# Three scheduling edits to a spectral-mixing and windowed-attention kernel: when the output projection's operands are prepared and where they live, which queue reads the row maxima, and the order in which a matrix piece is split

## The chip, the cores and the metric

One Trainium2 chip, one of its cores. The metric is device time in microseconds (us) of one execution. The times listed for the kernel before are 786.25, 770.50 and 777.87 us, median 777.87 us; the execution that was profiled took 772.52 us.

## What is computed (the reference, cut)

```python
# S = 2048 rows, D = 512 columns, 32 heads of 16, window W = 256
g = sigmoid((x * gate_w).sum(-1, keepdims=True))          # one gate per row
a = Cr @ (x @ Wr.T) - Ci @ (x @ Wi.T)                     # real part of a 2-D DFT
q, k, v = split(x @ wqkv)                                 # 32 heads
scores = (q @ k.T) * 16 ** -0.5                           # query i sees keys i-255 .. i
p = softmax(where(mask, scores, -1e9))
b = (p @ v) @ wo
out = g * a + (1 - g) * b
```

All of it is float32. A matmul of full precision is made of three in the faster float32r type: each operand is split into a high part (a cast) and a low part (operand minus high part), and high x high, high x low and low x high are accumulated (`TERMS`).

## The kernel before, in words

**One program order, written out by hand.** Every instruction is issued where the Python code calls it; each engine and each DMA queue works through its own instructions in that order. Two things are interleaved: the attention loop at the bottom of the function (`for n in range(N + LAG + 1)`), and a generator `dense()` that yields after each dense matmul (projections, then the DFT's products). `fill(n)` lets the generator advance by `rate / 2` steps, twice for each of the four head slots `p` of a turn `n`: 5 steps a turn once the projections are done (`FILL_SEQ`), 11 before (`FILL_PROJ`). Small work is postponed with `defer(ticks, fn, ...)`: a heap is emptied as a counter advances by 1 at each dense matmul, by 0.7 at each head slot, by 9 after each `pv`.

**The attention.** Heads come in 8 groups of 4, each with 16 row blocks, so 128 block turns. At turn `n` the kernel computes scores of block `n` (`s_head`, L442) and lets VectorE take the masked row maxima (L445); nine turns later (`LAG`), at `k = n - 9`, it computes the transposed scores (`t_head`, L497), in which the maxima are already subtracted because they sit as two extra rows (high and low part) in the tile `ring[0]`, and ScalarE exponentiates them (L498). GpSimd clears what lies outside the window (`t_mask`, L504 and L508). Every fourth turn `pv` multiplies by the values (L523), ScalarE copies one half of the sums out (L529), VectorE adds the other (L530). The scores of both kinds and these sums share four PSUM buffers (tag `st`).

**The row maxima's way.** Every fourth turn `m_rows(u)` (called here a unit, `u` counting from -3 to 29) splits 16 columns of maxima and transposes them on VectorE (L452 to L455); 2 ticks later SyncE's queue writes them to DRAM (`m_scr<-mt`), and 12 ticks after that reads them back as rows (`ring<-m_scr`, two or four DMAs a unit, 80 in all). In these 14 ticks falls the `pv` of the turn with its 9 ticks. Every load goes through `ld`, SyncE's queue (L97 in the profile); ScalarE issues a handful at the start only. DMAs take one of 8 semaphores in turn, so that each also waits for the landing of the one eight places before it.

**The normalizer's way.** After the last group of a half (groups 3 and 7) the sums and their row sums go out to DRAM (`o_out`), are packed (`o_pack`: `l_scr<-u_scr`, `o_scr<-u_scr`), the row sums read (`l_in`), inverted (`l_inv`) and written back (`l_back`), each step `d = 40` ticks after the one before. A set of four row blocks, 512 rows, is `sb` (0 to 3); the second half of `sb` is finished by `pv` 28 + `sb`, the last four of the attention.

**The DFT's last product.** 32 blocks, `c_block(n)`, each 12 matmuls with a piece of `cr` (n below 16) or `ci`. A piece is loaded three blocks ahead (`piece_load`: `raw`, `big`, and for odd rows `hl`) and split two blocks ahead (`piece_split`): the high part `hi` by ScalarE (L103), two differences on GpSimd (L328, L331) and one on VectorE, then the low part on GpSimd (L106), at ticks 0, 0, 2, 4 and 6. The differences feed only a check (`magnitudes`, L566; `guard`). The high part lies in a tile `es`, the low part in half of a tile `hl`.

**The output projection.** When the attention's loop is over, `attention_done` calls `o_prep(0)`: for each of four groups `o_load` reads inverted row sums (`rl<-l_scr`) and sums (`pt<-o_scr`), 256 KB each; 36 ticks later VectorE multiplies them (L830), ScalarE casts, VectorE subtracts. `o_prep(1)` comes 50 ticks later, `o_prep(2)` and `o_prep(3)` when `sb` 0 and 1 have been used. The results lie in the tiles `pt`, the products in `RL`, which takes the place of `ring[1]`. `wo` is loaded in four parts (`wo_load`): 0 and 1 at `n` = 18 and 19, 2 and 3 in `attention_done`. `wo_run` multiplies one of 16 row blocks (12 matmuls), once after each `c_block` if all is prepared, else at the very end.

## Time and profile before

| | before |
|---|---|
| median of the three times, us | 777.87 (770.50 to 786.25) |
| the profiled execution, us | 772.52 |
| its span (first to last instruction), us | 770.8 |
| mean granted clock of TensorE in it | 0.906 |
| instructions | 18841 |
| DMA: moved, mean rate | 174.36 MB, 226 GB/s |
| HBM read, written | 114.03 MB, 63.46 MB |

The profile names an engine's busy time (PE is TensorE, PEld its weight load, DVE VectorE, ACT ScalarE, POOL GpSimd, SPq the DMA queue of SyncE), and for a group or a single instruction the idle time before it with what ended it: `[3.75 <-DMA ring<-m_scr]` is 3.75 us of idling that ended when that DMA landed. Times in a timeline are us from the first instruction; tiles are written as what is written `<-` what is read. The attention's last matmuls run at 669 us; the first block of the DFT's last product begins at 353 us.

### The profile page before, as it was taken

Reading aid. Unit: us, or ns where it says so; the run is one execution under the profiler, and the core shown is the slowest. Engines: PE = TensorE matmul, PEld = TensorE weight load, DVE = VectorE, ACT = ScalarE, POOL = GpSimd, SP = SyncE. Lnnn points to the kernel's source line nnn. Section 1 sums busy time; section 2 is a strip of 40 time slices with the busy share of each in tenths; the row PEclk is TensorE's granted clock in tenths of the full one; section 3 lists DMA queues with packets and bytes.
Section 4 is the critical chain, followed back from the end, with each engine's and each line's share of the span. In section 5 each row is a group of like instructions: output and inputs, shape, how many; then the busy total and the mean of one; then the engine's idle time right before and its main releaser. Section 6 shows DMA issues by size and latency. Waiting matters only on the chain.

```text
span 770.8 us, 18841 instructions
## 1 busy us (share of the span) xinstructions
PE 650.1 (84%) x6558; PEld 499.8 (65%) x6558; DVE 544.1 (71%) x1471; ACT 437.8 (57%) x928; POOL 470.4 (61%) x718
## 2 busy tenths in 40 slices
PE   9999999899999999978677978878887687835976
PEld 6788887777788777766455655655555456624754
DVE  5388878898897889768567757676678863516554
ACT  6334775455576545666577657656756567514230
POOL 5002565667667878787768859796875869822000
PEclk9999999999999999989789879978978868975979
DMA  7857775777666877798868678885877648697675
GB/s 281 264 171 221 221 233 174 214 215 219 212 206 194 236 211 216 251 277 251 254 182 248 220 203 248 263 247 148 269 205 242 209 162 301 233 297 259 189 249 155
DMA packets 99994, 174.36 MB, mean 226 GB/s; under 512 B 34420, under 2 KB 35316, under 8 KB 99764
## 3 DMA queue, kind: packets, MB, share of 16 engines
q1 hardware_dynamic: 98452, 170.98, 72.2%
q10 hardware_dynamic: 1440, 2.10, 0.8%
q8 instruction: 54, 0.88, 0.5%
q14 instruction: 48, 0.39, 0.2%
HBM read 114.03 MB, written 63.46 MB: 230 GB/s over the span
## 4 chain that ended last, share of the span: by engine, by line
DMA 18%; PE 17%; POOL 8%; DVE 8%; issue 6%; SPq 4%; ACT 3%; DVEq 0%; POOLq 0%; ACTq 0%
DMA ring<-m_scr 5%; PE d L238 5%; SPq L97 4%; PE t L234 4%; DVE sm L445 3%; PE o L523 3%; DMA raw<-cr 3%; DMA ring<-qk_scr 3%; PE t L497 2%; DMA pt<-o_scr 2%; PE s L442 2%; POOL pt L504 1%; POOL hl L106 1%; DMA hl<-cr 1%; DMA ev<-wo 1%
## 5 line engine op out<-in xcount | busy, mean ns | idle before, releaser
L445 DVE CUSTOM_DVE_ANT_0 sm<-s,mask 128x384 f32<-128x384 f32 (+2 forms) x512 | 269.8, 527 | 87.0 <-PE s L442 41.9
L498 ACT ACTIVATE pt<-t 128x384 f32<-128x384 f32 (+2 forms) x512 | 234.2, 475 | 131.8 <-PE t L497 93.7
L497 PE MATMUL t<-ring,ring 50*128 50x384 f32 (+2 forms) x512 | 199.9, 400 | 56.6 <-DMA ring<-m_scr 32.0
L442 PE MATMUL s<-ring,ring 48*128 48x384 f32 (+2 forms) x512 | 185.0, 372 | 24.2 <-DVE nm L445 22.5
L504 POOL TENSOR_SCALAR_AFFINE_SELECT pt<-pt 128x256 f32<-128x256 f32 x256 | 116.0, 454 | 124.2 <-ACT pt L498 117.0
L238 PE MATMUL d<-big,hl 64*128 64x512 f32 x896 | 171.8, 421 | 0.0
L497 PEld LDWEIGHTS t<-ring,ring 50*128 50x128 f32 x512 | 101.9, 202 | 89.0 <-issue 26.5
L442 PEld LDWEIGHTS s<-ring,ring 48*128 48x128 f32 x512 | 99.4, 198 | 78.7 <-DVE nm L445 66.3
L238 PE MATMUL d<-hl,big 64*128 64x512 f32 x984 | 147.9, 395 | 0.0
L238 PE MATMUL d<-big,es 64*128 64x512 f32 x448 | 122.7, 473 | 0.0
L238 PEld LDWEIGHTS d<-big,hl 64*128 64x128 f32 x896 | 110.0, 198 | 5.2 <-issue 0.6
L238 PEld LDWEIGHTS d<-hl,big 64*128 64x128 f32 x984 | 105.2, 186 | 6.9 <-issue 0.8
L508 POOL TENSOR_SCALAR_AFFINE_SELECT pt<-pt 128x256 f32<-128x256 f32 x224 | 95.3, 425 | 0.0
L523 PE MATMUL o<-pt,vpad 64*32 64x320 f32 (+5 forms) x2816 | 83.3, 373 | 5.9 <-DVE nm L445 3.7
L523 PEld LDWEIGHTS o<-pt,vpad 64*32 64x32 f32 x2816 | 66.6, 113 | 28.1 <-DVE nm L445 10.3
L238 PEld LDWEIGHTS d<-big,es 64*128 64x128 f32 x448 | 66.3, 224 | 2.5 <-issue 0.6
L106 POOL TENSOR_TENSOR hl<-es,hl 128x512 fp32r<-128x512 f32 x14 | 19.0, 1359 | 65.2 <-ACT hl L103 61.6
L529 ACT COPY os<-o 128x512 f32<-128x512 f32 x32 | 18.8, 587 | 64.2 <-PE o L523 64.2
L530 DVE TENSOR_TENSOR os<-o,os 128x512 f32<-128x512 f32 x32 | 22.1, 690 | 42.8 <-ACT os L529 38.8
L106 POOL TENSOR_TENSOR hl<-raw,es 128x512 fp32r<-128x512 f32 x32 | 44.0, 1375 | 0.0
L243 ACT ACTIVATE es<-d 128x512 f32<-128x512 f32 x53 | 31.7, 598 | 19.8 <-PE d L238 19.0
L106 POOL TENSOR_TENSOR big<-big 128x512 fp32r<-128x512 f32 x32 | 41.6, 1304 | 0.2 <-ACT big L103 0.2
(100 smaller groups left out, 902.5 us busy)
## 6 DMA issues: line engine op xcount, KB each, us to landing
qk_scr<-hl SPq DMA_DIRECT2D x32, 512.0 KB
ring<-qk_scr SPq DMA_DIRECT2D x128, 128.0 KB
ring<-qk_scr SPq DMA_DIRECT2D x128, 64.0 KB
u_scr<-os SPq DMA_DIRECT2D x32, 256.0 KB
raw<-cr SPq DMA_DIRECT2D x16, 512.0 KB
big<-cr SPq DMA_DIRECT2D x16, 512.0 KB
raw<-ci SPq DMA_DIRECT2D x16, 512.0 KB
big<-ci SPq DMA_DIRECT2D x16, 512.0 KB
```

The source lines that it names most:

```text
L97: nc.sync.dma_start(dst, src)
L106: (nc.gpsimd if pool else nc.vector).tensor_sub(lo, raw, f(hi))
L234: nc.tensor.matmul(pss[0], w, x, start=start, stop=stop)
L238: nc.tensor.matmul(pss[h], w[r], x[r], start=start, stop=stop)
L243: nc.scalar.activation(t, pss[0], AF.Copy, scale=scale)
L442: nc.tensor.matmul(ps[:, :w], ring[0][r, p, jb * P:(jb + 1) * P], ring[1][r, p, k0:k0 + w], start=True, stop=True)
L445: nc.vector.tensor_tensor_reduce(out=sm[:, :w], in0=ps[:, :w], in1=mask[:, WIN - w:], scale=1.0, scalar=3e38, op0=OP.add, op1=OP.min, accu ...
L497: nc.tensor.matmul(ps[:, :w], ring[1][r, p, q0:q0 + P], ring[0][r, p, q0:q0 + w], start=True, stop=True)
L498: nc.scalar.activation(pt[:, j, :w], ps[:, :w], AF.Exp, scale=-1.0)
L504: nc.gpsimd.affine_select(a, a, pattern=[[0, 2], [1, P]], compare_op=OP.is_ge, fill=0.0, base=0, channel_multiplier=-1)
L508: nc.gpsimd.affine_select(a, a, pattern=[[0, 2], [-1, P]], compare_op=OP.is_gt, fill=0.0, base=0, channel_multiplier=1)
L523: nc.tensor.matmul(ot[h][32 * j:32 * j + 32, a - sb * 512:e - sb * 512], v2[r, j], pt[r, j, a - kb * P:e - kb * P], start=kb == kbs[0], st ...
```

## The change

1. The two or four reads of the maxima in each unit are issued by ScalarE's queue (`nc.scalar.dma_start`) instead of SyncE's.
2. In the second half of the normalizer's way the steps are 14 ticks apart instead of 40, and `l_back` calls `o_prep(sb)` at once. For `sb` 1 and 2 that waits until the attention is over; for `sb` 0 it happens in the attention, for `sb` 3 without a further condition.
3. `sb` 0 and 3 use tiles `big` for their results and `es` for the row sums; `sb` 1 and 2 keep `pt` and `RL`. The four groups of a set are loaded 9 ticks apart instead of 5, and multiplied 16 ticks after the load instead of 36.
4. All four parts of `wo` go into `big` tiles; parts 2 and 3 are loaded at `n` = 27 and 28. `wo_run` waits until all four have been split.
5. In `piece_split` the low part comes right after the high part (tick 2), the differences at ticks 4, 6 and 8; the high part lies in the other half of the `hl` tile, and `es` is free of it.

```diff
@@ m_rows, read
-                    ld(f(ring[0][64 * h + 48:64 * h + 50, :, b % NB * P:b % NB * P + (e - b) * P]),
-                       ms[:, h, :, o:o + e - b].rearrange("l p b i q -> l p (b i q)"))
+                    nc.scalar.dma_start(f(ring[0][64 * h + 48:64 * h + 50, :, b % NB * P:b % NB * P + (e - b) * P]),
+                                        ms[:, h, :, o:o + e - b].rearrange("l p b i q -> l p (b i q)"))
@@ pv
-        d = 40
+        d = 14 if hf else 40
...
             have.add(("o", sb, hf))
+            if hf:
+                o_prep(sb)
@@ piece_split
-        hi = ev.tile([P, 512], F32R, name="es", bufs=3)
         w = st.tile([P, 2, 512], F32R, name="hl")
+        hi = w[:, 1]
         defer(at_, hi_of, hi, main)
         for k, j in enumerate((2, 1, 3)):
             d, src, sign = left(i, tb, raws, j)
-            defer(at_ + step * k, minus if sign > 0 else plus, d, d, src, j != 3)
-        defer(at_ + step * 3, lo_of, w[:, 0], main, hi, True)
+            defer(at_ + step * (k + 2), minus if sign > 0 else plus, d, d, src, j != 3)
+        defer(at_ + step, lo_of, w[:, 0], main, hi, True)
@@ dense
-            if n in (18, 19):
-                wo_load(n - 18)
+            if n in (18, 19, 27, 28):
+                wo_load({18: 0, 19: 1, 27: 2, 28: 3}[n])
@@ wo_load
-        if g < 2:
-            t = big.tile([P, 2, 512], F32R, name="big")
-            d = [t[:, a] for a in range(2)]
-        elif g == 2:
-            d = [const.tile([P, 512], F32R, name=f"wo{a}", tag=f"vpad{a}") for a in range(2)]
-        else:
-            d = [const.tile([P, 512], F32R, name="wo2", tag="vpad2"), at.tile([P, 512], F32R, name="os", bufs=1)]
+        t = big.tile([P, 2, 512], F32R, name="big")
+        d = [t[:, a] for a in range(2)]
...
-        WO.append(d)
+        defer(34, WO.append, d)
@@ attention_done
-        o_prep(0)
-        defer(10, wo_load, 2)
-        defer(15, wo_load, 3)
-        defer(50, o_prep, 1)
         for tb in range(3):
-            defer(40, wo_get, tb)
+            defer(1 + 6 * tb, wo_get, tb)
@@ o_prep
-        if sb > 3:
-            return
-        if ("o", sb, 1) not in have:
+        if sb in (1, 2) and not FIN:
             return defer(6, o_prep, sb)
         OHL[sb] = []
         for g in range(NG):
-            defer(5 * g, o_load, sb, g)
+            defer(9 * g, o_load, sb, g)
@@ o_load
-        t = pt_tile([P, 3, 512], F32R)
         ls = l_scr[sb][g // 2]
-        rl = RL[0][:, sb % 2 * 2 + g // 2, g % 2]
+        if sb in (1, 2):
+            t = pt_tile([P, 3, 512], F32R)
+            rl, o = RL[0][:, sb % 2 * 2 + g // 2, g % 2], f(t[:, 2])
+        else:
+            t = big.tile([P, 2, 512], F32R, name="big")
+            rl, o = ev.tile([P, 512], F32, name="es", bufs=3), f(t[:, 1])
         ld(rl, bass.AP(tensor=ls.tensor, offset=ls[1, g % 2 * 8].offset, ap=[[512, 8], [0, 16], [1, 512]]))
-        ld(f(t[:, 2]), o_scr[sb][g])
+        ld(o, o_scr[sb][g])
...
-            nc.vector.tensor_mul(rl, f(t[:, 2]), rl)
+            nc.vector.tensor_mul(rl, o, rl)
...
-            defer(24, OHL[sb].append, t)
-        defer(36, product)
+            defer(8, OHL[sb].append, t)
+        defer(16, product)
@@ wo_run
-        if tb > 15 or len(OHL.get(sb, ())) < NG:
+        if tb > 15 or len(OHL.get(sb, ())) < NG or len(WO) < 4:
             return tick()
...
-        if c == 3:
-            o_prep(sb + 2)
```

## The prediction

> **What bounds the kernel now.** I read the page's busy times first, then a table by stage, then the waits, and last the timelines at the places where the change acts.
>
> ```profile
> span 770.8 us, 18841 instructions
> PE 650.1 (84%) x6558; PEld 499.8 (65%) x6558; DVE 544.1 (71%) x1471; ACT 437.8 (57%) x928; POOL 470.4 (61%) x718
> ```
>
> No engine is busy throughout, so the answer differs by stage. In the table a row is a stretch, its length, then the busy time of PE, PEld, DVE, ACT and POOL, the granted clock, the DMA engines' share and GB/s:
>
> ```profile
> 250.00:300.00 50.00, 46.09 (x563) 37.85 (x551) 42.62 (x114) 26.85 (x57) 41.31 (x64) 1.00 0.74 219
> 500.00:550.00 50.00, 39.54 (x349) 25.83 (x346) 37.06 (x103) 32.77 (x77) 38.99 (x57) 0.83 0.78 220
> 640.00:660.00 20.00, 14.03 (x159) 10.84 (x157) 6.02 (x7) 13.68 (x32) 18.15 (x25) 0.83 0.85 299
> 680.00:700.00 20.00, 6.47 (x14) 3.88 (x14) 3.46 (x6) 4.51 (x10) 7.51 (x6) 0.59 1.00 322
> ```
>
> While projections and attention run together, TensorE is the bound: 46.1 of 50 us, clock 1.00. In the second part every engine has slack and waits for another. At the attention's end GpSimd is the bound (18.2 of 20). Behind it TensorE does 6.5 us of work in 20 while the DMA engines are full. The waits name what the change addresses; the columns are us in total, times, longest:
>
> ```profile
> PE t L497 <- DMA ring<-m_scr: 32.0, 12, 7.0
> SPq L97 <- DMA m_scr<-mt: 18.6, 14, 3.2
> ```
>
> TensorE stood 32.0 us for maxima, all in the second part (the first such wait, 4.44 us, is quoted below), and SyncE's queue stood for the landing of the maxima's write before it could issue their read.
>
> **Term 1: the stretch behind the attention.** TensorE there (a bracket is the idle time before the row):
>
> ```profile
> 666.57 2.42 PE L523 MATMUL o<-pt,vpad 64*32 64x64 f32 x96
> ...
> 682.38 1.22 PE L234 MATMUL d<-big,es 128*128 128x512 f32 x2 [6.63 <-ACT es L103]
> 686.88 0.80 PE L234 MATMUL d<-big,hl 128*128 128x512 f32 x1 [3.27 <-POOL hl L106]
> ...
> 696.70 1.22 PE L234 MATMUL d<-big,es 128*128 128x512 f32 x2 [5.80 <-ACT es L103]
> 701.53 0.80 PE L234 MATMUL d<-big,hl 128*128 128x512 f32 x1 [3.61 <-POOL gl L618]
> ...
> 707.61 2.93 PE L234 MATMUL t<-big,pt 128*128 128x512 f32 x6
> ...
> 731.00 0.39 PE L234 MATMUL t<-wo,pt 128*128 128x512 f32 x1
> ...
> 742.00 2.76 PE L234 MATMUL t<-big,pt 128*128 128x512 f32 x6
> ...
> 754.04 0.79 PE L234 MATMUL t<-wo,pt 128*128 128x512 f32 x2 [0.38 <-DVE pt L106]
> ```
>
> Blocks 28 and 29 of the DFT run at once, 30 waits to 682.4 and 31 to 696.7 for their pieces; then eight blocks of the projection in 23.8 us (707.61 to 731.39, 2.97 each), then the ninth, which takes until 742.00. In blocks 30 and 31 the low part comes late, because GpSimd does two differences first:
>
> ```profile
> 681.75 1.27 POOL L331 TENSOR_TENSOR raw<-raw 128x512 f32<-128x512 f32 x1 [8.61 <-DMA raw<-ci]
> 683.82 1.77 POOL L328 TENSOR_TENSOR big<-big,hl 128x512 f32<-128x512 f32 x1 [0.81 <-DMA hl<-cr]
> 685.56 1.26 POOL L106 TENSOR_TENSOR hl<-raw,es 128x512 fp32r<-128x512 f32 x1
> ```
>
> - Low part first: waits of 3.27 and 3.61 shrink to about 1.3 (one GpSimd subtraction behind the cast): -4.3.
> - With `sb` 0 ready and part 3 of `wo` split 34 ticks after block 28 begins, the first `wo_run` that works stands at the end of block 30: 2.97 us fall into the wait for piece 31. -3.
> - `sb` 2 is loaded beside `sb` 1 right after the attention, some 40 us before its use. The ninth block took 10.6 us (731.39 to 742.00) and would take 2.97: -7.6. The smaller hold for `sb` 3 (0.38 in the last row, with the others about it some 1.4): -1.4.
> - Fewer restarts at the low clock (0.59 in that row): -2.7.
>
> The pieces come no sooner. SyncE's queue:
>
> ```profile
> 671.05 0.33 SPq L97 DMA_DIRECT2D u_scr<-os  x1
> ...
> 675.98 0.37 SPq L97 DMA_DIRECT2D raw<-ci  x1
> ...
> 687.52 0.36 SPq L97 DMA_DIRECT2D raw<-ci  x1
> ```
>
> The loads of `sb` 0 leave this place (2 MB, 6.5 us at 322 GB/s), but those of `sb` 1 and 2 now stand there, and `l_back` followed at once by `o_prep` makes the queue wait for the landing of `l_scr<-lt`. I count piece 30 as 2 to 3 us later, 31 unchanged. Sum -19; -30 if both pieces come with the freed bandwidth, -6 if they come later still.
>
> **Term 2: ScalarE waits for the write, first part.** The read stands 12 ticks behind the write, and nine of these are `pv`'s, so on ScalarE it falls one or two exponentials behind the copy of the `pv` sums. Unit 4 of 33, and with it the last of the 14 units that I followed between 76 and 309 us:
>
> ```profile
> 162.50 0.53 SPq L97 DMA_DIRECT2D m_scr<-mt  x1
> ...
> 166.04 0.55 SPq L97 DMA_DIRECT2D ring<-m_scr  x2
> ```
>
> ```profile
> 163.63 0.49 ACT L498 ACTIVATE pt<-t 128x384 f32<-128x384 f32 x1 [0.25 <-PE s L442]
> 164.72 0.49 ACT L498 ACTIVATE pt<-t 128x384 f32<-128x384 f32 x1 [0.59 <-PE t L497]
> ...
> 305.64 0.49 ACT L498 ACTIVATE pt<-t 128x384 f32<-128x384 f32 x1
> ```
>
> ```profile
> 166.52 0.34 PE L497 MATMUL t<-ring,ring 50*128 50x384 f32 x1
> ...
> 308.58 0.68 SPq L97 DMA_DIRECT2D ring<-m_scr  x2
> ```
>
> And of unit 13:
>
> ```profile
> 324.81 0.49 ACT L498 ACTIVATE pt<-t 128x384 f32<-128x384 f32 x1
> ...
> 333.97 1.55 SPq L97 DMA_DIRECT2D ring<-m_scr  x4
> ...
> 336.75 0.66 PE L497 MATMUL t<-ring,ring 50*128 50x384 f32 x1 [4.44 <-DMA ring<-m_scr]
> ```
>
> The queue read at 166.04, the moment the write had landed. ScalarE would be at the read at 164.12 and stand until 166.0, issue for 0.5, and start at 166.5 the exponential that began at 164.72. TensorE's scores at 166.52, which need a PSUM buffer that a later exponential frees, come at 168.2: 1.6 us late. In the last unit ScalarE is there at 306.13 and waits to 308.5. Over the 14 units it waits 29 us, and TensorE's next scores come 24 us late. Unit 13 adds a wait of 8.7 us (325.3 to 334.0) and unit 14 one of about 5, of which TensorE keeps some 9, since it stands there for 4.4 us already. So 33; VectorE, 42.6 of 50, uses the pauses to catch up, and 3.9 us of idling in 50 is all that can be made up from. I take 25, bounds 8 and 43 (the upper with a lowered clock behind each pause).
>
> **Term 3: the maxima land sooner, second part.** Of the 32.0 us, 26 lie behind 355 us. Two reads on today's queue, from the chain of waits, bound a landing:
>
> ```profile
> 394.26 5.55 DMA ring<-m_scr
> ...
> 473.27 1.59 DMA ring<-m_scr
> ```
>
> ```profile
> 504.37 0.81 ACT L498 ACTIVATE pt<-t 128x384 f32<-128x384 f32 x2
> ...
> 507.76 0.57 SPq L97 DMA_DIRECT2D ring<-m_scr  x2
> ```
>
> ```profile
> 515.00 0.66 PE L497 MATMUL t<-ring,ring 50*128 50x384 f32 x1 [3.75 <-DMA ring<-m_scr]
> ```
>
> In unit 22 ScalarE is free at 505.2, the write has landed by 506.5, and a read of 1.6 us is there before 509: the 3.75 us vanish. But ScalarE runs late in this part, and in half of these units it reaches the read 1 to 4 us behind SyncE's queue. At 1.6 us a landing, 17 of the 26 us go; at 5.55 none, and some 4 are added. With the loads of a DFT piece just ahead of it on the one queue and none on the other, the short landing is nearer. Since what follows meets the next wait (32.8 and 39.0 of 50 us on ACT and POOL), -14; bounds -25 and +4.
>
> The Trainium skill speaks against this term: "DMA: Bandwidth & Descriptors", section "Issuing engines are not separate DMA queues", says that issuing from several engines saves only the sequencer's time to start a transfer, as all run on the same 16 DMA engines. By that the reads land as late as now and the sum is 14 higher. The same page, section "Queues, rings and completion order", has each engine alternate between queues packet by packet, which speaks for the short landing; no row here decides.
>
> **Term 4: what is added in the attention.** For `sb` 0 eight loads (2 MB), four products and low parts on VectorE, four casts on ScalarE, and SyncE's queue waits for `l_scr<-lt` and for the fourth `es` tile. VectorE has room there (6.0 of 20 us), which hides them; GpSimd has none (18.2 of 20), and its subtraction took 1.77 instead of 1.27 us beside VectorE (683.82 above). With the DMA at 0.85 already, +4; 0 to 10. The differences that now come later delay ScalarE's `magnitudes` by a subtraction; that is in it. The other edits (tiles, `d`) cost nothing of their own.
>
> **Sum.** -19 + 25 - 14 + 4 = -4 on the profiled execution's 772.5 us (1.7 of it outside the span): 768.5 us. The median of the runs shown, 777.9, lies 5.4 higher, so I count from the profiled one, which is near the lowest.
>
> **Rivals.**
> - *ScalarE's wait is mostly absorbed.* Once delayed, it meets the writes later, and VectorE, which sets when they are written, has caught up. Term 2 falls to 8, term 3 reaches -18, term 1 -21, term 4 +3: 744.5 us. For: in the second part ScalarE mostly comes after the landing. Against: the rows of unit 4, with VectorE not behind.
> - *Slower: ScalarE's wait in front of the exponentials decides.* Place: the read behind `pv`. Price: 43 in term 2, and shorter waits in the second part become ScalarE's (-8). With -15 and +6: 798.5 us. It decides once TensorE's pauses pass 2 us a unit, so that the clock falls, 1.00 until now. For: TensorE has 3.9 us of slack in 50. By the Trainium skill, "TensorE: Matmul & The Clock Gate", Part 1, an idle window of about 3.4 us halves the clock; the trace agrees as far as it goes (0.83 where waits reach 7.0 us, 1.00 where there are none), and pauses of 2 us would be too short for it.
> - *The reads land as late as before* (term 3 at 0): 782.5 us.
> - *The tail doesn't do what it says*: the loads of `sb` 1 and 2 push piece 31 and the projection back as those of `sb` 0 and 1 do now; term 1 at -6: 781.5 us.
>
> **How the numbers follow.** Forecast 0.40, the rivals in order 0.26, 0.16, 0.11, 0.07. A measurement of this kernel tells about 2% from no change: below 757.1 or above 788.0 us. Faster: 0.06 of the forecast, 0.24 of the first rival and 0.02 of the others, 0.32. Slower: 0.13 of the second, 0.03 of the third and 0.02 of the rest, 0.18. Same: 0.50. The range reaches to the first rival and near the second, 744 to 796; the forecast's own is 757 to 780.
>
> **What would show it.** Right: in the changed profile the attention's last `pv` comes near 683 us instead of 667; up to 350 us "ACT pt <- DMA m_scr" or ScalarE's queue waits near 29 us; "PE t <- DMA ring<-m_scr" falls below 15; from the start of the last `pv` to the end 85 us instead of 104, the ninth projection block without a hold. Wrong: the last `pv` not later than 670 (term 2), that wait still at 26 or more (term 3), or block 31 later than 700 us after a shift by the attention (term 1).

## The result, and the profile after

| | before | after |
|---|---|---|
| median, us | 776.82 (same session) | 813.35 (809.94 to 813.96) |
| the profiled execution, us | 772.52 | 809.94 |
| its span, us | 770.8 | 807.9 |
| granted clock of TensorE | 0.906 | 0.873 |

The change makes the kernel slower: ratio 1.049, 95% interval [1.0416, 1.0563]. The forecast was 768.5 us in 744 to 796, and the result lies outside. Medians here and below are over all executions of a kernel, ratios leave out those in the slower state that some executions show.

Where the time went shows in the starts of `pv`, the first L523 row of each unit in TensorE's timeline. They are equal points of the program in both kernels:

| start of `pv` number | 0 | 5 | 10 | 13 | 14 | 15 | 20 | 25 | 31 | end of the span |
|---|---|---|---|---|---|---|---|---|---|---|
| after minus before, us | +2.6 | +10.2 | +19.8 | +23.3 | +34.7 | +35.9 | +33.4 | +37.9 | +42.7 | +37.1 |

The loss is made in the first part (35 us by `pv` 14); behind `pv` 14 another 8 come, and the stretch behind the last `pv` gives 5.5 back (104.2 to 98.7). The stages between `pv` 0, 14 and 31 (columns as in the prediction), first of before, then of the changed kernel:

```profile
87.50:344.96 257.46, 237.85 (x2920) 199.17 (x2919) 214.58 (x631) 158.08 (x335) 184.13 (x294) 0.99 0.73 220
344.96:666.57 321.61, 254.59 (x2706) 178.13 (x2705) 220.80 (x608) 208.73 (x478) 250.65 (x381) 0.85 0.76 229
```

```profile
90.11:379.66 289.55, 249.02 (x2919) 204.37 (x2918) 215.46 (x633) 155.78 (x335) 183.75 (x294) 0.95 0.66 202
379.66:709.23 329.57, 267.01 (x2706) 191.83 (x2705) 225.78 (x615) 212.87 (x477) 252.73 (x379) 0.79 0.75 224
```

The work is the same in both, so a stage's length splits into TensorE's idling (length minus busy time) and its busy time. Of the 32.1 us that the first stage grows, 20.9 are idling and 11.2 are the same matmuls taking longer, at a granted clock of 0.95 instead of 0.99. In the second stage TensorE idles 4.5 us less than before, and its matmuls take 12.4 us more, at 0.79 instead of 0.85.

The waits name the idling (us in total, times, longest), first one of before, then the changed kernel's:

```profile
PE t L497 <- ACT pt L498: 10.0, 15, 2.1
```

```profile
PE t L497 <- ACT pt L498: 40.5, 24, 9.8
ACT pt L498 <- DMA ring<-m_scr: 28.4, 12, 4.4
PE t L497 <- DMA ring<-m_scr: 16.1, 8, 3.4
ACT hl L103 <- DMA ring<-m_scr: 10.6, 1, 10.6
...
ACT ev L243 <- DMA ring<-m_scr: 4.3, 1, 4.3
```

TensorE's wait for the maxima halved, from 32.0 to 16.1 us, which is what the edit is about. But ScalarE, which issues the read, now stands 45.2 us (28.4 + 10.6 + 4.3, and one wait of 1.9) in front of it, and TensorE's wait for ScalarE's exponentials is 40.5 us, 24 times; before it was 10.0 us, 15 times. How one such wait looks, in unit 4 again, first on SyncE's queue, then on ScalarE:

```profile
170.70 0.53 SPq L97 DMA_DIRECT2D m_scr<-mt  x1
```

```profile
171.02 0.59 ACT L529 COPY os<-o 128x512 f32<-128x512 f32 x1 [1.65 <-PE o L523]
171.85 0.49 ACT L498 ACTIVATE pt<-t 128x384 f32<-128x384 f32 x1 [0.24 <-PE s L442]
174.42 0.54 ACTq L468 DMA_DIRECT2D ring<-m_scr  x2
175.06 0.49 ACT L498 ACTIVATE pt<-t 128x384 f32<-128x384 f32 x1 [2.71 <-DMA ring<-m_scr]
```

ScalarE is free at 172.34 and can issue the read only at 174.42, when the write begun at 170.70 has landed; the exponential behind it runs 2.71 us late. In unit 13 the write itself is late, because SyncE's queue takes 7.3 us to issue eight loads ahead of it (SyncE's queue, then ScalarE):

```profile
346.16 7.30 SPq L97 DMA_DIRECT2D ring<-qk_scr  x8
...
354.93 0.58 SPq L97 DMA_DIRECT2D m_scr<-mt  x1
```

```profile
348.11 0.49 ACT L498 ACTIVATE pt<-t 128x384 f32<-128x384 f32 x1
357.92 1.20 ACTq L468 DMA_DIRECT2D ring<-m_scr  x4
359.22 0.62 ACT L103 CAST hl<-es 128x512 fp32r<-128x512 f32 x1 [10.62 <-DMA ring<-m_scr]
```

That wait falls into the step of 11.4 us between `pv` 13 and 14 (11.6 in a kernel below in which ScalarE waits and no read has moved). A stretch that the prediction showed:

```profile
250.00:300.00 50.00, 45.49 (x510) 38.85 (x511) 38.11 (x110) 25.21 (x55) 35.60 (x57) 0.93 0.61 191
```

Between 250 and 300 us TensorE does 510 matmuls instead of 563, ScalarE and GpSimd are less busy, and the clock is 0.93 instead of 1.00 (the program stands some 15 to 20 us earlier at these times than before). The stretch behind the attention, TensorE's timeline:

```profile
709.23 2.37 PE L523 MATMUL o<-pt,vpad 64*32 64x64 f32 x88
...
729.78 5.98 PE L234 MATMUL d<-big,hl 128*128 128x512 f32 x12 [8.14 <-ACT hl L103]
735.58 2.24 PE L234 MATMUL t<-big 128*128 128x512 f32 x9
745.53 0.80 PE L234 MATMUL t<-big 128*128 128x512 f32 x1 [7.71 <-ACT big L103]
...
748.00 5.09 PE L234 MATMUL d<-big,hl 128*128 128x512 f32 x12
758.21 0.19 PE L628 MATMUL t<-gl 128*1 128x1 f32 x2 [5.12 <-DVE gl L623]
758.32 10.58 PE L234 MATMUL t<-big 128*128 128x512 f32 x36
768.75 21.92 PE L234 MATMUL t<-big,pt 128*128 128x512 f32 x96
790.50 11.19 PE L234 MATMUL t<-big 128*128 128x512 f32 x60
```

and its first 20 us by stage:

```profile
709.20:729.20 20.00, 10.77 (x125) 7.99 (x124) 10.33 (x11) 6.52 (x15) 8.23 (x7) 0.82 0.98 315
```

The projection now runs without a hold: 15 blocks in 43.4 us, from 758.32 to 801.7, where the kernel before took 57.1 us for 16 (707.61 to 764.7). But it begins later, counted from the last `pv`: 49.1 us instead of 41.0.

### The profile page after: what moved, and what is told of

Its sections match the earlier page's. It is cut to its first block, busy times and chain, and to the rows that moved or that the text cites. A ratio compares the mean times of both kernels' runs of the same rounds, so it can differ in the third digit from the quotient of the medians.

```text
span 807.9 us, 18862 instructions
## 1 busy us (share of the span) xinstructions
PE 671.2 (83%) x6558; PEld 521.2 (65%) x6558; DVE 546.9 (68%) x1471; ACT 436.3 (54%) x928; POOL 474.8 (59%) x718
## 4 chain that ended last, share of the span: by engine, by line
PE 22%; DMA 20%; DVE 6%; issue 4%; POOL 4%; ACT 4%; SPq 3%; ACTq 0%; DVEq 0%; POOLq 0%
PE d L238 8%; PE t L234 5%; DMA ring<-qk_scr 4%; PE t L497 3%; DMA ring<-m_scr 3%; PE o L523 3%; SPq L97 3%; PE s L442 3%; DMA rl<-l_scr 2%; DVE sm L445 2%; DMA m_scr<-mt 1%; ACT pt L498 1%; DMA u_scr<-os 1%; DMA ev<-r_scr 1%; DMA big<-ci 1%
## 5 line engine op out<-in xcount | busy, mean ns | idle before, releaser
L445 DVE CUSTOM_DVE_ANT_0 sm<-s,mask 128x384 f32<-128x384 f32 (+2 forms) x512 | 270.5, 528 | 92.0 <-PE s L442 46.4
L238 PE MATMUL d<-big,hl 64*128 64x512 f32 x1344 | 294.4, 461 | 0.5 <-DVE es L246 0.5
L497 PE MATMUL t<-ring,ring 50*128 50x384 f32 (+2 forms) x512 | 213.2, 424 | 73.1 <-ACT pt L498 40.5
L442 PE MATMUL s<-ring,ring 48*128 48x384 f32 (+2 forms) x512 | 194.3, 388 | 28.6 <-DVE nm L445 18.8
L238 PEld LDWEIGHTS d<-big,hl 64*128 64x128 f32 x1344 | 185.6, 220 | 8.3 <-issue 1.3
L497 PEld LDWEIGHTS t<-ring,ring 50*128 50x128 f32 x512 | 109.1, 215 | 109.4 <-ACT pt L498 61.7
L442 PEld LDWEIGHTS s<-ring,ring 48*128 48x128 f32 x512 | 106.5, 210 | 83.5 <-DVE nm L445 58.8
L238 PE MATMUL d<-hl,big 64*128 64x512 f32 x984 | 154.9, 405 | 1.0 <-ACT es L243 0.7
L508 POOL TENSOR_SCALAR_AFFINE_SELECT pt<-pt 128x256 f32<-128x256 f32 x224 | 95.6, 427 | 0.0
L523 PE MATMUL o<-pt,vpad 64*32 64x320 f32 (+5 forms) x2816 | 80.3, 365 | 4.4 <-POOL pt L504 2.3
L523 PEld LDWEIGHTS o<-pt,vpad 64*32 64x32 f32 x2816 | 64.4, 111 | 26.4 <-DVE nm L445 8.2
L106 POOL TENSOR_TENSOR hl<-raw,hl 128x512 fp32r<-128x512 f32 x39 | 50.0, 1281 | 32.4 <-ACT hl L103 27.6
L530 DVE TENSOR_TENSOR os<-o,os 128x512 f32<-128x512 f32 x32 | 22.1, 691 | 40.3 <-ACT os L529 37.0
L246 DVE SCALAR_TENSOR_TENSOR es<-d,es 128x512 f32<-128x512 f32 x53 | 36.4, 687 | 17.2 <-ACT es L243 16.7
L445 DVE DVE_READ_ACCUMULATOR2_ANT nm<- 128x1 f32 x512 | 42.3, 83 | 0.0
```

The source lines that it names most:

```text
L106: (nc.gpsimd if pool else nc.vector).tensor_sub(lo, raw, f(hi))
L238: nc.tensor.matmul(pss[h], w[r], x[r], start=start, stop=stop)
L246: nc.vector.scalar_tensor_tensor(t, pss[1], scale, t, op0=OP.mult, op1=OP.add)
L442: nc.tensor.matmul(ps[:, :w], ring[0][r, p, jb * P:(jb + 1) * P], ring[1][r, p, k0:k0 + w], start=True, stop=True)
L445: nc.vector.tensor_tensor_reduce(out=sm[:, :w], in0=ps[:, :w], in1=mask[:, WIN - w:], scale=1.0, scalar=3e38, op0=OP.add, op1=OP.min, accu ...
L497: nc.tensor.matmul(ps[:, :w], ring[1][r, p, q0:q0 + P], ring[0][r, p, q0:q0 + w], start=True, stop=True)
```

## The experiments

All were compared with the kernel before on the same chip, whose medians there were 774 to 776 us. "Shift" is the start of a `pv` against the kernel before.

**One part at a time.** First the changed kernel with only the reads put back on SyncE's queue:

```diff
-                    nc.scalar.dma_start(f(ring[0][64 * h + 48:64 * h + 50, ...
+                    ld(f(ring[0][64 * h + 48:64 * h + 50, ...
```

> The kernel after the change with one part undone: the maxima are read by SyncE's queue again. Theory W (ScalarE's wait for the write of the maxima, in front of its exponentials, is what made the kernel slower): the attention's last pv comes back from 709 to about 670 us, the stretch behind it stays near 99 us, so about 770 us in all, level with the kernel before. Rival P (what was put into the attention, the preparation of the first rows and the earlier normalizer, slows it): the last pv stays above 695 us and the time above 795 us.

778.02 us, ratio 1.012 [0.998, 1.026]; last `pv` at 673.6 us, 98.3 us from there to the end. So most of the loss hangs on the queue of the reads. The reverse, the kernel before with the reads alone moved (the same lines the other way):

> The kernel before with only the reads of the maxima moved to ScalarE's queue. Theory W: the last pv moves from 667 to about 703 us (the shift is there by unit 14 and does not come back), stretch behind it unchanged at 104 us, so about 808 us. Rival P: within 10 us of the kernel before. If the reads land sooner and that is worth what was predicted, the shift shrinks by 10 us or more between pv 15 and pv 28.

807.47 us, ratio 1.044 [1.032, 1.057]. Shifts +12.5 at `pv` 6, +22.9 at 13, +35.2 at 14, +33.4 at 31. The first part costs all of it; from `pv` 14 to the last it gets 1.8 us back, not 14. Next, the kernel before with item 5 of the change alone (low parts first, the high part in the `hl` tile):

```diff
-            defer(at_ + step * k, minus if sign > 0 else plus, d, d, src, j != 3)
-        defer(at_ + step * 3, lo_of, w[:, 0], main, hi, True)
+            defer(at_ + step * (k + 2), minus if sign > 0 else plus, d, d, src, j != 3)
+        defer(at_ + step, lo_of, w[:, 0], main, hi, True)
```

> The kernel before with only the order in piece_split changed (low part right behind the high part). Both theories: the attention within 5 us; the two waits for the low part behind the attention (3.3 and 3.6 us) shrink to about 1, so 4 us less, 768 us. If ScalarE's sums of magnitudes, now behind one more subtraction of GpSimd, cost something, the attention is later by that.

785.44 us, ratio 1.020 [1.008, 1.031]: not the gain of 4 us that was expected. The edit costs some 10 us by the medians (7 in the trace, all of it inside the attention), and the stretch behind the attention is 104.0 us, as before. The two waits for the low part there did shrink, from 3.27 and 3.61 us to 0.18 and 0.19; but block 31 waits 8.46 us for the high part of its piece (before 5.80), and the guard's matmul 4.79 us (before 1.32). Last, the preparation of the projection alone (items 2 to 4 of the change, with the high part in the `hl` tile):

```diff
-        d = 40
+        d = 14 if hf else 40
...
+            if hf:
+                o_prep(sb)
...
-            if n in (18, 19):
+            if n in (18, 19, 27, 28):
...
-            defer(5 * g, o_load, sb, g)
+            defer(9 * g, o_load, sb, g)
...
-        defer(36, product)
+        defer(16, product)
```

> The kernel before with only the preparation of the projection changed (first rows inside the attention, own places, wo parts 2 and 3 earlier, shorter steps). Theory W: last pv at 667 to 672 us, the stretch behind it about 102 us, in all 770 to 775 us. Rival P: last pv above 690 us and more than 795 us.

769.44 us, ratio 0.997 [0.992, 1.002]; last `pv` at 667.4 us, 99.7 us from there to the end. By the ratios the three parts measured alone give +4.4%, +2.0% and -0.3%, together 6.1%; the whole change gave 4.9%. The single intervals are 0.5 to 1.3 points to either side, so they add up as far as these runs can tell; the -0.3% is not told from nothing.

**ScalarE's wait, or the reads' way?** The reads stay on SyncE's queue; ScalarE issues one more read of 128 bytes, into a tile that nobody uses, at the same place:

```diff
         def read():
+            nc.scalar.dma_start(seen[u % 2:u % 2 + 1], ms[0, 0, 0, 0, 0:1])
```

> The kernel before, with its reads of the maxima on SyncE's queue as before, but with one more transfer of 128 bytes from the maxima's scratch into a tile that nobody reads, issued by ScalarE at the place where the read is issued. ScalarE thus waits for the write as in the change, and no read that TensorE needs has moved. Theory W (the loss is ScalarE standing for the write, not the way the reads travel): about 803 us, the last pv near 695 us. Theory Q (the loss comes from the reads themselves on the other queue, landing later or costing more to issue): about 777 us, the last pv near 667.

802.57 us, ratio 1.038 [1.029, 1.048]; shifts +11.3 at `pv` 6, +18.6 at 13, +30.2 at 14, +31.1 at 31, nearly those of the moved reads. ScalarE in unit 4 of this kernel:

```profile
171.59 0.49 ACT L500 ACTIVATE pt<-t 128x384 f32<-128x384 f32 x1 [0.25 <-PE s L443]
174.66 0.22 ACTq L464 DMA_DIRECT2D seen<-m_scr  x1
174.98 0.49 ACT L500 ACTIVATE pt<-t 128x384 f32<-128x384 f32 x1 [2.90 <-DMA m_scr<-mt]
```

A transfer that moves nothing of use costs 27 us, because the in-order engine that issues it has to stand until what it reads has been written. The opposite test moves the reads, but 24 ticks behind the write instead of 12:

```diff
-            defer(12, read)
+            defer(24, read)
```

> The kernel before with the reads on ScalarE's queue, but 24 ticks behind the write instead of 12. Theory W: the write has landed when ScalarE comes to the read in nearly all units, its waits fall from some 45 us to below 10, and the time returns to about 780 us (the later reads may cost TensorE a few us in the second part). Theory Q: still about 800 us. If the shorter landing that the prediction counted on existed, the wait of TensorE for the maxima would fall below 15 us and the time to about 765 us.

796.61 us, ratio 1.031 [1.021, 1.040]. In some units of the second part these reads come behind the first scores that take the maxima, so those subtract maxima of other rows; the work is the same. The first part confirms the theory: shift +0.6 at `pv` 9, where the 12 ticks cost 15.0. In the second part 24 ticks are too late: TensorE waits 38.4 us for the maxima. That is not because the reads travel long: issued so late, the reads of one unit land in a median of 2.4 us there (units 14 to 29), on the queue on which they took 4.2 us in the changed kernel. So the next kernel has 24 ticks only while the projections run:

```diff
-            defer(12, read)
+            defer(12 if "proj" in have else 24, read)
```

> The kernel before with the reads on ScalarE's queue, 24 ticks behind the write while the projections run, and 12 as in the change behind them. In the first part ScalarE then no longer stands for the write (with 24 ticks throughout, the start of the pv of unit 9 was only 0.6 us later than before, against 15.0 with 12), so what is left is the second part alone, in which the prediction counted on -14 (term 3). If the reads land as late as on SyncE's queue: TensorE's wait for the maxima stays near 26 us or more, the last pv comes between 667 and 680 us (unit 13's wait for a late write is left), and the time is 777 to 788 us. If they land as soon as predicted: that wait below 15 us, the last pv near 655 to 660, about 767 us.

780.59 us, ratio 1.006 [1.002, 1.010]: with ScalarE's wait gone from the first part, the loss is 6 us instead of 32. What is left arises in the step at `pv` 14 (unit 13's late write, +8.0) and in one of 3.6 at `pv` 10 (a step of 5.0 us stands there in a version with unmoved reads too, the first with a repaired stretch below). The second part of this kernel is the test of term 3. Its waits from `pv` 15 to the last, first of before, then of this kernel, last of the kernel with the read of 128 bytes, in which the real reads are on SyncE's queue:

```profile
PE t L497 <- DMA ring<-m_scr: 26.4, 10, 7.0
...
PE t L497 <- DVE os L530: 4.8, 14, 1.0
```

```profile
PE t L497 <- DMA ring<-m_scr: 14.7, 9, 3.4
...
PE t L497 <- DVE os L530: 13.4, 15, 4.1
```

```profile
PE t L499 <- DMA ring<-m_scr: 9.0, 6, 3.9
```

The wait for the maxima fell by 11.7 us, but the stretch from `pv` 15 to `pv` 31 took 302.8 us, and before 303.5. TensorE now stands 13.4 us for a PSUM buffer that VectorE's addition of the `pv` sums frees (L530), before 4.8; in all it idles 3.3 us less there, and its matmuls take 2.6 us more. The last fence shows that a smaller wait for the maxima is no sign of reads that land sooner: where the reads were not moved at all and only ScalarE was held up in front of them, it fell to 9.0 us, and that stretch took 305.1 us.

**Low parts first, with its consumers moved too.** If ScalarE stands in front of its `magnitudes` for differences that now come later, moving them by the same two steps should repair it:

```diff
-            defer(at_ + step * (5 + k), magnitudes, sums[...], d, d)
+            defer(at_ + step * (7 + k), magnitudes, sums[...], d, d)
```

> The kernel before with the low parts first, and with ScalarE's sums of magnitudes two steps later as well, so that the order on ScalarE fits GpSimd's new order again. If the 7 us that low parts first cost inside the attention are ScalarE standing in front of its magnitudes for GpSimd's differences, the last pv comes near 667 us instead of 674, the waits of ScalarE for GpSimd fall back, and the time is about 774 us. If they come from GpSimd's later masks or from the shared tile, the time stays near 784 us.

787.88 us, ratio 1.024 [1.015, 1.033]: not the repair that was expected. ScalarE's waits for GpSimd in front of its `magnitudes` (L566) did fall, between 350 and 680 us from 14.6 us with the low parts first alone (first fence) to 5.8 (second), without any gain:

```profile
ACT raw L566 <- POOL raw L331: 7.1, 5, 2.5
ACT raw L566 <- POOL raw L328: 4.9, 4, 2.1
...
ACT raw L566 <- POOL big L328: 2.6, 1, 2.6
```

```profile
ACT raw L566 <- POOL big L328: 2.6, 1, 2.6
ACT raw L566 <- POOL raw L331: 1.9, 3, 1.4
...
ACT raw L566 <- POOL raw L328: 1.3, 3, 0.7
```

Why low parts first costs 10 to 12 us is therefore not settled. Two things narrow it down. The shared tile is not the cause: the preparation alone has the high part in the `hl` tile too, and costs nothing. And the loss is not idling of TensorE: between `pv` 14 and 31 it idles 65.8 us with the low parts first and 66.7 in this kernel, before 67.0; but its matmuls take 6.5 and 9.1 us more, at a granted clock of 0.81 and 0.83 instead of 0.85. What lowers the clock is open, and a version below without this order (rows issued by GpSimd) has a stage of that kind too (+7.9 us at 0.80), so single traces don't tie it to the edit.

**The stretch behind the attention.** Three kernels on top of the preparation alone were to take away the holds seen in the changed kernel. The core of the first:

```diff
-            if n in (18, 19, 27, 28):
+            if n in (18, 19, 26, 27):
...
+        late = 2 if n > 28 else 0
...
-            defer(at_ + step * k, minus if sign > 0 else plus, d, d, src, j != 3)
-        defer(at_ + step * 3, lo_of, w[:, 0], main, hi, True)
+            defer(at_ + step * (k + late), minus if sign > 0 else plus, d, d, src, j != 3)
+        defer(at_ + step * (1 if late else 3), lo_of, w[:, 0], main, hi, True)
...
-        defer(8, total, c[3])
+        defer(60, total, c[3])
...
-            wo_run()
+            for _ in range(3 if n == 30 else 1):
+                wo_run()
...
-        if sb in (1, 2) and not FIN:
+        if sb in (1, 2) and not (FIN and (sb == 1 or ("piece", 31) in have)):
```

> The preparation part of the change alone (maxima read by SyncE as before), with the four things repaired that held the stretch behind the attention in the changed kernel: parts 2 and 3 of wo loaded at pieces 26 and 27 instead of 27 and 28, so that part 3's cast stands ahead of piece 31's; low parts first for pieces 29 to 31 alone; three blocks of the projection instead of one in the wait for piece 31; the guard's matmul 60 ticks behind its VectorE work instead of 8; and sb 2's rows loaded once piece 31's loads are issued. If the missed term 1 was these holds, the stretch from the last pv to the end falls from 99.7 to about 87 us and the time to about 757 us. If the stretch is set by the full DMA engines, it stays within 3 us of 99.

770.15 us, ratio 0.993 [0.988, 0.998]; the stretch 95.6 us. That is between the two expectations. The holds at `wo` shrank to one of 1.31 us (4.85 and 2.83 in the preparation alone). In front of the guard's matmul TensorE still stands 3.50 us, now for an eviction by VectorE, and other holds of 2.4 to 4.4 us came between 700 and 736 us.

The second spreads the loads otherwise:

```diff
-            for _ in range(3 if n == 30 else 1):
+            for _ in range(2 if n == 30 else 1):
...
+        if sb == 3 and ("rows", 2) not in have:
+            return defer(6, o_prep, sb)
...
-            defer(9 * g, o_load, sb, g)
+            defer((4 if sb in (1, 2) else 9) * g, o_load, sb, g)
...
-        defer(16, product)
+        defer(30 if sb else 16, product)
```

> The repaired stretch behind the attention once more, where VectorE stood for rows that had not landed: two blocks of the projection in the wait for piece 31 instead of three, sb 1 and 2 loaded 4 ticks apart instead of 9, the products 30 ticks behind their loads instead of 16, and sb 3 loaded behind sb 2 instead of before it. If the holds of 0.8 to 4.4 us that the last version still had between 700 and 736 us were products in VectorE's order in front of the evictions, the stretch falls from 95.6 to about 86 us and the time to about 757 us; if the transfers themselves are late, it stays above 92 us.

769.91 us, ratio 0.995 [0.990, 0.999]; 101.4 us in its trace, so above 92, with one hold of 9.7 us in which TensorE waits for an eviction by VectorE. With the reads moved, late in the first part, on top of this version:

```diff
-                    ld(f(ring[0][64 * h + 48:64 * h + 50, ...
+                    nc.scalar.dma_start(f(ring[0][64 * h + 48:64 * h + 50, ...
...
-            defer(12, read)
+            defer(12 if "proj" in have else 24, read)
```

> The version with the repaired stretch, and the reads on ScalarE's queue, 24 ticks behind the write while the projections run and 12 behind them. Its difference to that version is the worth of the moved reads without ScalarE's wait: within 8 us of it either way if the landing is as late as on SyncE's queue, 10 us or more faster if term 3 was right.

780.17 us, ratio 1.007 [1.002, 1.012]: some 10 us slower than the version without moved reads. In the traces it is 4.0 us behind that version by `pv` 13 and 12.2 by `pv` 14, in front of which ScalarE stands 8.9 us for the late write of unit 13; from `pv` 15 to 31 it takes 308.2 us, against 311.9. So it is still ScalarE's wait that costs, and behind it the moved reads gain 3.7 us in this pair of traces.

The third goes back to the order of loads of the preparation alone and changes, against the first:

```diff
-            for _ in range(3 if n == 30 else 1):
+            for _ in range(2 if n == 30 else 1):
...
-        if sb in (1, 2) and not (FIN and (sb == 1 or ("piece", 31) in have)):
+        if sb in (1, 2) and not FIN:
...
-            rl, o = ev.tile([P, 512], F32, name="es", bufs=3), f(t[:, 1])
+            o = f(t[:, 1])
+            rl = RL[0][:, 2 + g // 2, g % 2] if sb else ev.tile([P, 512], F32, name="es", bufs=3)
```

> The preparation part alone once more (maxima read by SyncE, sb 1 and 2 loaded right behind the attention, products 16 ticks behind their loads, as in the change), with the holds taken away one by one: parts 2 and 3 of wo at pieces 26 and 27, low parts first for pieces 29 to 31 alone, two blocks of the projection in the wait for piece 31, the guard's matmul 60 ticks behind its VectorE work, and the fourth sum of sb 3 no longer in a tile that SyncE's queue waits for. Counted from the preparation part's own trace (block 31 could start at 704.5 us instead of 709.6, one more projection block of 2.9 us ahead of it, 3.2 us at the guard): the stretch from the last pv to the end 99.7 - 5 - 3 - 3 = about 89 us, and 758 to 762 us. If the holds only move on, as in the two versions before, it stays above 94 us and the time near 769 us.

770.95 us, ratio 0.995 [0.989, 1.001]; stretch 96.2 us: the holds only moved on. Here TensorE had done four projection blocks by 696 us and then waited 13.45 us for the piece of block 31, which began 43.4 us behind the last `pv`. Two more kernels ask what holds that piece. First, the rows of `sb` 1 and 2 behind it in the queue:

```diff
-        if sb in (1, 2) and not FIN:
+        if sb in (1, 2) and not (FIN and ("piece", 31) in have):
```

> The last version (stretch behind the attention repaired, maxima read by SyncE), but the rows of sb 1 and sb 2 are issued only once the loads of piece 31 have been. In that version piece 31's load was issued 35.2 us behind the last pv and block 31 began 43.4 us behind it, with 16 transfers of rows (4 MB) issued ahead of it on the same queue. If those rows are what holds piece 31, block 31 begins about 30 us behind the last pv; the stretch is 96 less some 8 us if the projection then finds its rows in time, and as long as before if the rows are now the late ones. If piece 31 is held by its own buffers or by the DMA engines as such, block 31 stays near 43 us.

781.92 us, ratio 1.009 [1.005, 1.013]. In it the row sums of `sb` 3 take the places of those of `sb` 1 too early, which changes values and no work. TensorE's timeline:

```profile
666.22 2.37 PE L523 MATMUL o<-pt,vpad 64*32 64x64 f32 x88
...
695.02 2.99 PE L234 MATMUL d<-big,hl 128*128 128x512 f32 x12
709.93 1.92 PE L234 MATMUL t<-big,pt 128*128 128x512 f32 x3 [11.91 <-ACT pt L103]
718.56 1.22 PE L234 MATMUL t<-big,pt 128*128 128x512 f32 x2 [6.71 <-ACT pt L103]
```

Block 31 begins 28.8 us behind the last `pv` instead of 43.4, without any wait, and then the projection waits 11.9 and 6.7 us for the rows; the stretch is 109.2 us. Second, the rows at their old places, but issued by GpSimd:

```diff
-        ld(rl, bass.AP(tensor=ls.tensor, ...
-        ld(o, o_scr[sb][g])
+        q = nc.gpsimd if sb in (1, 2) else nc.sync
+        q.dma_start(rl, bass.AP(tensor=ls.tensor, ...
+        q.dma_start(o, o_scr[sb][g])
```

> The same version with the rows of sb 1 and sb 2 issued by GpSimd at the old places, so that SyncE's queue holds the pieces, the sums and the results alone. If the order of issue on the one queue is what holds piece 31 (it waits behind transfers that wait), it is issued some 8 us sooner although the same bytes move. If it is the bytes, it lands no sooner: block 31 stays about 43 us behind the last pv.

776.43 us, ratio 1.003 [0.998, 1.008]. Piece 31's load is issued 25.9 us behind the last `pv` instead of 35.2, and its first part (`raw<-ci`) lands after 34.5 us instead of 42.7, as the order theory says: with the same bytes to move it comes 8 us sooner. Block 31 begins 46.4 us behind the last `pv` all the same, because of a new cost. GpSimd stands up to 4.2 us in front of a row it issues, its low parts and differences come behind that, and ScalarE casts piece 31 only after a sum of magnitudes that waited 8.02 us for such a difference:

```profile
720.24 1.06 ACT L568 ACTIVATE big<-big 128x1024 f32<-128x1024 f32 x1 [8.02 <-POOL big L328]
...
723.29 0.62 ACT L103 CAST hl<-raw 128x512 fp32r<-128x512 f32 x1
```

So the place in SyncE's queue does hold piece 31. But none of these orders gained: with the pieces first the rows are late, with the rows first the pieces, and with the rows on GpSimd the splitting.

## Why the prediction was wrong, by its own steps

- **The size of each miss.** Counted at `pv` 14, `pv` 31 and the end, the forecast was +25, -10 (terms 3 and 4) and -19; measured +34.7, +8.0 and -5.5. All three failed to the slow side, by 9.7, 18 and 13.5 us.
- **Term 2 (+25; measured +34.7 at `pv` 14 in the whole change, +35.2 with the reads moved alone).** Place and mechanism were right: in unit 4, which was worked through, ScalarE was forecast to stand 1.9 us and stood 2.1; up to 350 us it stood 29.8 us in all, forecast 29; and the wait alone, without the moved reads, costs 27. What failed is the size. The deduction of 8 us for VectorE catching up stands against a loss of 34.7 where 33 had been worked out, and that 33 was met partly by luck: of the 32.1 us between `pv` 0 and 14 only 20.9 are added idling of TensorE, and 11.2 are longer matmuls at a lower clock, which the prediction had in the upper bound alone. Units 13 and 14 were put at 9 together; the step from `pv` 13 to 15 is 12.6.
- **Term 3 (-14; measured about 0: -1.8 from `pv` 14 to 31 with the reads moved alone).** This is the largest step that failed. It assumed that a read on a queue of its own lands in 1.6 us, and that TensorE's waits for it, once gone, are time gained. The chain of waits of the changed kernel and of the one with 24 ticks while the projections run shows the landings, with no projection traffic left:

```profile
427.02 3.63 DMA ring<-m_scr
486.84 4.73 DMA ring<-m_scr
...
683.81 2.25 DMA ring<-m_scr
```

```profile
403.21 4.07 DMA ring<-m_scr
...
635.21 5.29 DMA ring<-m_scr
```

  Over units 14 to 29, from the issue of a unit's first read to the landing of its last, the medians are 5.0 us before, 4.2 after and 4.9 with 24 ticks; from the issue of the write to the landing of the rows 9.4, 10.3 and 9.8 us. A single read lands some 0.7 to 1 us sooner (medians 4.4 us before, 3.4 and 3.7). But ScalarE comes to the first read later than SyncE's queue did (2.2 us behind the write's landing, before 1.6), and has other work between the reads of a unit, so what the queue saves is lost again. TensorE's wait did fall to 16.1 and 14.8 us (the mark was 15), and nothing was gained: the second half of the assumption failed by itself. With 24 ticks TensorE stood for VectorE's sums instead (13.4 us, before 4.8); in the whole change it stood for ScalarE's exponentials (15.5 us behind `pv` 15, before 8.6), and its matmuls ran at a lower clock. By the Trainium skill, "DMA: Bandwidth & Descriptors", section "Issuing engines are not separate DMA queues", transfers of several engines share the same 16 DMA engines, and issuing from another one saves only the sequencer's time. These medians agree in the main, with landings of 4.2 and 4.9 us where 1.6 was expected. The prediction weighed that rule as a rival (reads land as late as before, chance 0.16) and chose against it.
- **Term 1 (-19; measured -5.5).** The projection's own part came out: its run to the end shrank from 63.2 to 49.6 us (-13.6, where block in the wait, ninth block, `sb` 3 and clock were put at -14.7). What failed is that the rest would gain 4.3: block 31 and the guard ended 8 us later instead, and block 31 began at 705.3 us when the shift of 42.7 is taken off, past the 700 that was named as a sign of being wrong. Pieces 30 and 31 were issued 12.2 and 26.1 us behind the last `pv` (before 9.4 and 21.0), since the rows of `sb` 1 and 2 stand ahead of them; piece 31 landed after 35.0 us instead of 29.4. Part 3 of `wo` was split behind piece 31's cast (the hold of 7.71), and the guard's matmul stood 5.12 us for VectorE. The prediction's rival for this (-6) had the mechanism; it got 0.07.
- **Term 4 (+4).** The preparation alone shifts the last `pv` by +0.8 us, so the loads and products in the attention cost next to nothing. What was wrong is the half sentence that low parts first is inside it: alone that edit costs some 10 us, and its -4.3 in term 1 did not appear in its own trace (104.0 us against 104.2), because the waits behind the shortened ones grew by as much.
- **The rivals.** The slower one (ScalarE's wait decides, 798.5 us, price 43 with a lowered clock) named what happened, but it still counted on shorter waits in the second part (-8) and on -15 in term 1. No single rival had terms 1 and 3 fail together with it, and they did. The lowered clock that it named was about a third of the loss by `pv` 14 (11.2 of 32.1 us). The prediction called pauses of 2 us too short for it; but in the changed kernel the granted clock is 0.50 from 271.4 to 278.2 us, and the longest pause of TensorE in the 30 us before that is 1.54 us, ending at 270.59. That is one place in one trace; in the kernel before, pauses of up to 1.83 us left the clock at 1.00 up to `pv` 13.

Left open: what lowers the clock in the second part of the changed kernel and with the low parts first; and how much of the stretch behind the attention is set by the DMA engines' rate (in its first 20 us they are busy for 0.98 of the time at 315 GB/s) and how much by order. The fastest version found, the preparation alone with its first repairs, is 0.7% faster than before (0.2 to 1.2%); the versions next to it, at 0.995 to 0.997, are not told apart from it.

## What to carry to other kernels

A DMA issued by a compute engine stands in that engine's order: where it had to wait for a write, the exponential behind it waited too (2.71 us in unit 4). So put it where the data has certainly arrived, or leave it on a queue that has nothing else to do. A wait that shrinks is not time gained until the engine's whole idle time and its clock have been read from the same stage (here -11.7 us of one wait, -3.3 us of idling, -0.7 us of time). Behind the attention, with the DMA engines 0.88 to 0.98 busy in the first 20 us, a load moved forward moved another one back.

## What the runs showed that was not expected

- One 128-byte read a unit, issued by ScalarE 12 ticks behind the write, costs nearly as much as all moved reads (27 us against 32 by the medians).
- In units 14 to 29 the reads of one unit, 8 KB each and less, took 1.9 to 7.1 us to land on SyncE's queue and 1.8 to 7.5 on ScalarE's. Their size does not set it: single reads of 8 KB took 1.6 to 6.8 and 1.5 to 5.2 us.
- Issued by GpSimd, a 256 KB row load occupies it 0.56 to 0.78 us, and GpSimd stood 2.3 to 4.2 us in front of several of them:

```profile
699.11 0.63 POOL L826 DMA_DIRECT2D rl<-l_scr  x1 [4.22 <-issue]
699.73 0.56 POOL L827 DMA_DIRECT2D pt<-o_scr  x1
```
